# One order table for all engines through batches 0 and 1 of a retention and gated-MLP kernel; q scaled into a buffer of its own, chunk loads in three parts, fixed buffers

## The chip, the core and the metric

The kernel runs on one core of one Trainium2 chip. A core has a matmul engine (TensorE; PE in the profile, its weight loads PEld), a vector engine (VectorE; DVE), an activation engine (ScalarE; ACT), a general engine (GpSimd; POOL) and a sequencer that issues the transfers (SyncE; SP). Each works through its own queue of instructions in order and waits on semaphores for the others. The metric is the time of one execution in microseconds (us), less is better.

## What is computed

Eight batches of 576 positions. First retention: causal scores of eight heads with a decay per head, times v. Then a gated MLP whose gate mixes the positions.

```python
def _attn_ref(q, k, v):                        # [8, 8, 576, 64] each
    scores = scale * np.matmul(q, k.transpose(0, 1, 3, 2))
    gamma = 1.0 - 2.0 ** (-5.0 - np.arange(H))
    rel = pos[:, None] - pos[None, :]
    Dmat = np.where(rel >= 0, gamma[:, None, None] ** rel, 0.0)
    return np.matmul(scores * Dmat, v)
def _moe_ref(x, w_in, w_spatial, b_spatial, w_out):   # x [8, 576, 512]
    h = np.maximum(x @ w_in, 0.0)
    u, v = h[..., :512], h[..., 512:]
    v_n = (v - mean(v)) / np.sqrt(var(v) + 1e-06)
    v_s = np.einsum('ts,bsd->btd', w_spatial, v_n) + b_spatial[None, :, None]
    return (u * v_s) @ w_out
```

## The kernel before

**Precision.** Every wide matmul operand is split into a rounded fp32r part (hi) and a remainder (lo), and a product is three matmuls (`mm3`: hi·hi, hi·lo, lo·hi). The weights arrive as 64-bit floats, seen as pairs of 32-bit words. One block of 128x512 weights takes an absolute value on ACT and a clamp (`front`), three bit operations on DVE (`mid_steps`: shift and mask, two `scalar_tensor_tensor`), a rounding copy on ACT and a subtraction (`back`). There are twelve such blocks: kind 1 (the v half of w_in, by rows), kind 0 (the u half, by columns) and kind 2 (w_out). The spatial weights are split by `w_sp_steps`.

**Stages of a batch.** Retention goes in four chunks of 128 positions and a tail of 64. A chunk has 16 `scores` matmuls (k times q), which DVE multiplies with the decay mask (`mask`, tile `at`); 16 `update` matmuls (k scaled times v), which with POOL's `decay` become the states `sh` and `st`; and `carried` (states times scaled q) and `values` (masked scores times v), which add up in one pair of PSUM banks (`r`). `evac_hi` (ACT) and `evac_lo` (DVE) split that into `x`. Then v (five row blocks, 56 matmuls of 128x512, each with relu, mean and variance on DVE, and a split: tile `vn`), u (96 matmuls of 128x288), vs (112: spatial weights times vn, times u, split into g) and f (96: g times w_out, stored). All but retention share four rotating PSUM banks (`ps_m`, `bufs=4`).

**Scaling.** `prep` multiplies q by `qs` and k by `kd` on POOL, in place; scores and carried both read the scaled q, and the mask holds the inverse power. So scores wait for both multiplications.

**What sets the order.** Up to line 712 every engine follows program order: the calls from line 550 on are the order for batch 0 and part of batch 1, and each engine's queue is that program's instructions for it. A `front`, `prep`, `burst` or `go(v[i])` puts its instructions on several engines at once, so that they stand in one and the same order on all. From line 712 a list scheduler orders the rest; `interleave` (line 530) deals out retention of batch b+1 among the stages of batch b. `load` fetches a chunk of q, k twice (two layouts) and v as one transfer of 1 MB into one of two rotating buffers (chunks 2 and 3 of batch 0 borrow the places of `u` and `wout0`); all transfers are issued by SP in one queue. `spin` runs matmuls on zeros while the first data is under way.

Of the kernel before, what the change touches and what calls it, by code (L numbers as in the profile page):

```python
# [9 lines left out]
F32 = mybir.dt.float32  # L10
# [21 lines left out]

@with_exitstack
def retention_gmlp(ctx, tc, qkv, tails, w_in, w_sp, b_sp, w_out, amask, tmask, qscale, kdec, sdec, out):
    nc = tc.nc
    cp = ctx.enter_context(tc.tile_pool(name="cp", bufs=1))
    ld = ctx.enter_context(tc.tile_pool(name="ld", bufs=2))
    wk = ctx.enter_context(tc.tile_pool(name="wk", bufs=2))
    sp = ctx.enter_context(tc.tile_pool(name="sp", bufs=1))
    ps_r = ctx.enter_context(tc.tile_pool(name="ps_r", bufs=1, space=PSUM))  # L40
    ps_m = ctx.enter_context(tc.tile_pool(name="ps_m", bufs=4, space=PSUM))
# [16 lines left out]
    def slot(name):  # L58
        return cp.tile([P, 2, NCB, S], F32R, name=name, tag="slot", bufs=2)
# [32 lines left out]

    def spin(name, n):
        ps = ps_m.tile([P, 512], F32, name=name, tag="m")
        for i in range(n):
            pe.matmul(ps, idle[:, :P], idle, start=True, stop=True)
# [7 lines left out]
    spin("idle0", 12)  # L104

    tail = {}

    def load(b, c):
        if b == 0 and c in (2, 3):
            tag = ("u", "wout0")[c - 2]  # L110
            t = cp.tile([P, NDB, S] if c == 2 else [P, NDB, DM], F32, name=f"qkv_{b}_{c}", tag=tag)
            t = t.rearrange("p a n -> p (a n)")[:, :4 * 512].rearrange("p (a n) -> p a n", a=4)
        else:
            t = ld.tile([P, 4, 512], F32, name=f"qkv_{b}_{c}", tag="qkv")
        q, k = (t[:, i].rearrange("p (a n) -> p a n", a=NP) for i in range(2))
# [12 lines left out]
    def load_tail(b):
        t = ld.tile([P, 3, NP * TL], F32, name=f"tail_{b}", tag="tail", bufs=1)
        dma(t, tails[b])  # L130
        q, k = (t[:, i].rearrange("p (a n) -> p a n", a=NP) for i in range(2))
        tail[b] = q, k, t[:, 2]

    staged = {}
    early = cp.tile([P, NCB, DH], F32, name="early", tag="vn0")
    raw_v = slot("raw_v").bitcast(I32).rearrange("p i a n -> p (i a n)")

    def fetch(kind, i):
# [3 lines left out]
        else:  # L142
            t = sp.tile([P, 1024], I32, name=f"raw_{kind}{i}", tag="raw", bufs=4)
# [4 lines left out]
    def fetch_wsp():  # L148
        w = slot("raw_s").bitcast(F32).rearrange("p i a n -> p (i a) n")
        for sb in range(NC):  # L150
            dma(w[:, sb], w_sp[sb * P:(sb + 1) * P, :])
        for i in range(2):
            dma(w[i * TL:(i + 1) * TL, NC], w_sp[NC * P:, :])
        dma(w[TL:TL + 1, NC + 1], b_sp)
        staged["s"] = w

    load(0, 0)
    for i in range(2, NCB):
        fetch(1, i)
    dma(sd, sdec)  # L160
    load(0, 1)
    load(0, 2)
    load(0, 3)
    dma(amt, tmask)
    load_tail(0)
    po.memset(vt2.bitcast(F32), 1.0)
    po.memset(wtl[1][TL:].bitcast(F32), 0.0)

    def split(hi, lo, src, eng):
        ac.copy(out=hi, in_=src)  # L170
        eng.tensor_tensor(out=lo, in0=src, in1=hi.bitcast(F32), op=ALU.subtract)

    part = {}

    def front(kind, i, clamp=po):
        words = staged[kind, i].rearrange("p (n two) -> p n two", two=2)
        hw, lw = words[:, :, 1], words[:, :, 0]
        f = early[:, i] if kind == 1 else sp.tile([P, 512], F32, name=f"f_{kind}{i}", tag="f", bufs=3)
        a = f if clamp is po else ps_m.tile([P, 512], F32, name=f"w_{kind}{i}", tag="m")
        ac.activation(out=a, in_=hw.bitcast(F32), func=AF.Abs)  # L180
        if clamp is po:
            po.tensor_scalar(out=a, in0=a, scalar1=2.0 ** -15, scalar2=None, op0=ALU.max)
        part[kind, i] = hw, lw, a, f

    def mid_steps(kind, i):
        hw, lw, a, f = part[kind, i]
        direct = kind == 1 and a is not f
        ps = a if kind != 1 or direct else ps_m.tile([P, 512], F32, name=f"w_{kind}{i}", tag="m")
        part[kind, i] = f, ps
        fi = ps.bitcast(I32)  # L190
        if direct:
            ve.tensor_scalar(out=a, in0=a, scalar1=2.0 ** -15, scalar2=None, op0=ALU.max)
        ve.tensor_scalar(out=fi, in0=a.bitcast(I32), scalar1=3, scalar2=0x3FFFFFFF, op0=ALU.logical_shift_left, op1=ALU.bitwise_and)
        ve.scalar_tensor_tensor(out=fi, in0=hw, scalar=-2 ** 30, in1=fi, op0=ALU.bitwise_and, op1=ALU.bitwise_or)
        yield
        ve.scalar_tensor_tensor(out=fi, in0=lw, scalar=29, in1=fi, op0=ALU.logical_shift_right, op1=ALU.bitwise_or)
        yield

    def mid(kind, i):
        for _ in mid_steps(kind, i):  # L200
            pass

    def back(kind, i, eng=po):
        hi, lo = (w[:, i, DH:] if kind == 1 else w[:, :, i * P:(i + 1) * P] for w in (win if kind < 2 else wout))
        f, ps = (t if kind == 1 else t.rearrange("p (a n) -> p a n", a=NCB) for t in part[kind, i])
        ac.copy(out=hi, in_=ps)
        if eng is po and kind == 1:
            ac.copy(out=f, in_=ps)
        eng.tensor_tensor(out=lo, in0=f if eng is po else ps, in1=hi.bitcast(F32), op=ALU.subtract)

    def w_sp_steps():
        w = staged["s"]
        for sb in range(NC):
# [24 lines left out]

    def prep(b, c):
        q, _, kn, _ = chunk[b, c]  # L240
        q = q.rearrange("p a (s n) -> p a s n", s=2)
        po.tensor_tensor(out=q, in0=q, in1=qs.rearrange("p a (s n) -> p a s n", s=1).broadcast_to([P, NP, 2, D]), op=ALU.mult)
        kh = kn.rearrange("p (h d) -> p h d", h=H)
        po.tensor_tensor(out=kh, in0=kh, in1=kd.broadcast_to([P, H, D]), op=ALU.mult)

    def prep_tail(b):
        q = tail[b][0]
        po.tensor_tensor(out=q, in0=q, in1=qs, op=ALU.mult)
# [23 lines left out]
    def carried(b, c, flip):  # L272
        q = chunk[b, c][0]
# [5 lines left out]
        if c == NC - 1:  # L279
            q = tail[b][0]  # L280
# [21 lines left out]
    def mask(b, c):  # L302
        a = wk.tile([P, 2, NP, D], F32, name=f"at_{b}_{c}", tag="at")
        ve.tensor_tensor(out=a, in0=sc, in1=am, op=ALU.mult)
        at[b, c] = a
# [484 lines left out]
```

## Time and profile before

| | us |
|---|---|
| median of 3 runs (lowest, highest) | 580.56 (580.24, 580.73) |
| the profiled execution's own time | 578.85 |
| its span | 577.1 |
| PE busy in the span | 532.2 (92%), 7247 matmuls |
| DVE, ACT, POOL busy | 244.8, 210.7, 163.0 |
| mean granted PE clock | 0.958 |
| chain of waits that ended last | PE 78%, POOL 8%, DVE 5%, DMA 3% |

An engine that is busy is not always at its full rate: a matmul that runs at half clock is twice as long and just as busy. So PE is read together with its granted clock, and its work is counted in matmuls times their duration at full clock. The profile's tables by stage give both for any stretch.

### The profile page before, as it was taken

The page shows a single profiled execution, that of the slowest core. Times are in us where ns is not written, and L with a number is a line of the kernel's source. Part 1 is how long each engine was busy: PE and PEld are TensorE (multiplying, and loading weights), DVE is VectorE, ACT ScalarE, POOL GpSimd, SP SyncE. Part 2 cuts the span into 40 slices and gives each one's busy share as a digit, 9 for nine tenths or more (in the row PEclk, how much of TensorE's full clock was granted, in tenths as well). Part 3 has the DMA queues.
Part 4 walks back from the last instruction along what each step waited for, and adds up shares of the span by engine and source line. Part 5 has one row for each costly group of instructions (what it writes and reads, how often), then busy time and mean ns, then how long its engine had stood idle before and what let it go on. Part 6 is the DMA issues. An engine that isn't in the chain of part 4 may idle for free.

```text
span 577.1 us, 16334 instructions
## 1 busy us (share of the span) xinstructions
PE 532.2 (92%) x7247; PEld 493.9 (86%) x7247; DVE 244.8 (42%) x586; ACT 210.7 (37%) x479; POOL 163.0 (28%) x173
## 2 busy tenths in 40 slices
PE   5366886898998999999999999999999999999997
PEld 4365676887997989999899989998999989998997
DVE  4524542477034255341735164533734073515350
ACT  3213551256222246223722255223622264225522
POOL 4541765575014232122222322220222222000000
PEclk8577887999999999999999999999999999999999
DMA  8590124510113452222222522242212422010002
GB/s 307 231 352 10 64 76 137 174 49 1 51 40 141 145 188 75 74 88 98 74 76 74 183 75 75 76 141 84 73 48 83 164 76 74 2 64 21 1 1 83
DMA packets 21449, 55.49 MB, mean 96 GB/s; under 512 B 2305, under 2 KB 14849, under 8 KB 17410
## 3 DMA queue, kind: packets, MB, share of 16 engines
q1 hardware_dynamic: 21378, 54.44, 26.9%
q8 instruction: 57, 0.93, 0.7%
q14 instruction: 14, 0.11, 0.1%
HBM read 45.00 MB, written 9.44 MB: 94 GB/s over the span
## 4 chain that ended last, share of the span: by engine, by line
PE 78%; POOL 8%; DVE 5%; DMA 3%; issue 2%; ACT 2%; SPq 0%; ACTq 0%; POOLq 0%; DVEq 0%
PE vs L72 19%; PE f L72 18%; PE u L72 15%; PE v L72 14%; PE r L72 13%; POOL qkv L72 4%; DVE f L72 2%; DMA qkv<-in_qkv 2%; DMA raw_v<-in_w_in 1%; POOL f L72 1%; POOL dec L72 1%; ACT x L72 1%; DVE x L72 1%; DVE st L72 1%; POOL win L72 1%
## 5 line engine op out<-in xcount | busy, mean ns | idle before, releaser
L72 PE MATMUL vs<-wsp,vn 128*128 128x288 f32 x768 | 117.8, 300 | 1.8 <-ACT pre L72 1.8
L72 PEld LDWEIGHTS vs<-wsp,vn 128*128 128x128 f32 x768 | 106.8, 190 | 3.9 <-ACT pre L72 2.0
L72 PE MATMUL u<-x,win 128*128 128x288 f32 x768 | 107.0, 299 | 2.5 <-ACT u L72 2.4
L72 PEld LDWEIGHTS u<-x,win 128*128 128x128 f32 x768 | 104.5, 191 | 4.0 <-ACT u L72 2.7
L72 PE MATMUL v<-win,x 128*128 128x512 f32 x384 | 94.3, 401 | 0.0
L72 PE MATMUL f<-g,wout 128*128 128x288 f32 x672 | 92.8, 296 | 1.0 <-issue 1.0
L72 PEld LDWEIGHTS f<-g,wout 128*128 128x128 f32 x672 | 89.9, 188 | 1.5 <-issue 0.9
L72 PEld LDWEIGHTS v<-win,x 128*128 128x128 f32 x384 | 72.0, 190 | 17.1
L72 POOL TENSOR_TENSOR dec<-sh,sd 128x256 f32<-128x256 f32 x32 | 19.6, 613 | 220.4 <-DVE sh L72 163.6
L72 PE MATMUL r<-qkv 64*64 64x64 f32 x2048 | 43.6, 233 | 26.2 <-POOL qkv L72 25.1
L72 PEld LDWEIGHTS r<-qkv 64*64 64x64 f32 x2048 | 38.2, 146 | 29.8 <-POOL qkv L72 28.8
L72 DVE BATCH_NORM_STATS2 s<-v 128x6 f32<-128x512 f32 (+1 forms) x40 | 27.7, 692 | 71.7 <-ACT v L72 68.2
L72 POOL TENSOR_TENSOR qkv<-qkv,qs 128x512 f32<-128x512 f32 x32 | 41.0, 1282 | 51.7 <-DMA qkv<-in_qkv 42.4
L72 DVE TENSOR_TENSOR vs<-vs,u 128x288 f32<-128x288 f32 x56 | 26.0, 464 | 57.5 <-PE vs L72 57.4
L72 ACT CAST g<-vs 128x288 fp32r<-128x288 f32 x56 | 22.4, 400 | 75.0 <-DVE vs L72 75.0
L72 ACT COPY o<-f 128x288 f32<-128x288 f32 x64 | 25.6, 400 | 62.4 <-PE f L72 57.8
L72 DVE TENSOR_TENSOR at<-r,am 128x512 f32<-128x512 f32 x32 | 22.0, 688 | 59.9 <-PE r L72 59.8
L72 ACT CAST x<-r 128x512 fp32r<-128x512 f32 x32 | 18.7, 586 | 69.4 <-PE r L72 39.9
L72 ACT ACTIVATE u<-u 128x288 f32<-128x288 f32 x56 | 22.8, 407 | 38.5 <-PE u L72 38.3
L72 DVE TENSOR_TENSOR g<-vs,g 128x288 fp32r<-128x288 f32 x56 | 25.5, 456 | 23.0 <-ACT g L72 19.8
L72 DVE TENSOR_TENSOR x<-r,x 128x512 fp32r<-128x512 f32 x32 | 21.9, 685 | 31.5 <-ACT x L72 31.5
L72 POOL TENSOR_TENSOR qkv<-qkv,kd 128x512 f32<-128x512 f32 x32 | 33.4, 1043 | 0.1
(82 smaller groups left out, 615.1 us busy)
## 6 DMA issues: line engine op xcount, KB each, us to landing
qkv<-in_qkv SPq DMA_DIRECT2D x31, 1024.0 KB, 5.0
out<-o SPq DMA_DIRECT2D x64, 144.0 KB, 1.8
tail<-in_tails SPq DMA_DIRECT2D x8, 384.0 KB, 7.0
raw_v<-in_w_in SPq DMA_DIRECT2D x4, 512.0 KB, 6.7
raw<-in_w_in SPq DMA_DIRECT2D x4, 512.0 KB, 9.8
raw<-in_w_out SPq DMA_DIRECT2D x4, 512.0 KB, 3.5
raw_s<-in_w_sp SPq DMA_DIRECT2D x4, 288.0 KB, 3.3
qkv<-in_qkv SPq DMA_DIRECT2D x2, 512.0 KB, 6.6
```

Source lines behind the costliest of these rows:

```text
L72: ins = op(*args, **kw)
```

## The change

The calls that ordered batches 0 and 1 are gone. All their work, with retention of batches 0, 1 and 2 and the first steps of batch 3's, is cut into 188 chains (`scores_chain`, `state_chain`, `burst_chain`, `v_chain`, `weight` and so on), and a string `ORDER` of 612 words names, word by word, which chain takes its next step. A step is mostly one operation on one engine, so the engines' queues are no longer tied to one another call by call. A word also says which engine does a step that either POOL or DVE can do (`w.1.2.vv`: clamp and subtraction on DVE). A string `BANKS` says which of the four PSUM banks each tile of this part gets. From batch 2 on the scheduler and `interleave` work as before.

Further: `prep_q` writes the scaled q to a buffer `qsc`, so that scores read q as it was loaded, and the mask (`am`) now holds the decay of the difference; for a batch's first chunk only the half that is needed is scaled. A chunk's transfer is three (q and k, k by position, v), into two, two and three fixed buffers, and it is issued one chunk earlier. A weight block's last bit operation writes from PSUM to an SBUF tile, from which the rounding copy and the subtraction read; the extra ACT copy of `back` is gone. All tiles are allocated once by name (`keep`); tags that were shared by rotation are now named places (`lent`).

```diff
+ORDER = """
+    D.1.0 z.0.12 D.1.2 d.0.0 d.0.0 w.1.0.vp w.1.0.vp c.a c.k w.1.0.vp D.1.1 w.1.2.vv g.0.0 d.0.0 k.0.0.p c.q
...
+BANKS = "012301320103012130230230030230202123123132323020121312002131232123102313"
...
+    def keep(name, shape, dtype=F32, tag=None):
+        if name not in kept:
+            kept[name] = cp.tile(shape, dtype, name=name, tag=tag or name)
+        return kept[name]
...
+            n = b * NC + c + (0 if b else 2)
+            qk = keep(f"qk{n % 2}", [P, 2, 512])
+            kn = keep(f"kn{n % 2}", [P, 512])
+            vv = keep(f"vv{n % 3}", [P, 512])
...
+            parts = (qk, qkv[b, c, :, :2]), (kn, qkv[b, c, :, 2]), (vv, qkv[b, c, :, 3])
...
+        ve.scalar_tensor_tensor(out=f.bitcast(I32), in0=lw, scalar=29, in1=fi, op0=ALU.logical_shift_right, op1=ALU.bitwise_or)
+        yield
+        ac.copy(out=at_hi(), in_=form(f))
+        yield
+        last.tensor_tensor(out=at_lo(), in0=form(f), in1=at_hi().bitcast(F32), op=ALU.subtract)
...
+    def prep_q(b, c, eng=po):
+        q = chunk[b, c][0].rearrange("p a (s n) -> p a s n", s=2)
+        t = keep(f"qsc{c % 2}", [P, NP, 2, D])
...
+        r = slice(1 if c == 0 else 0, 2)
+        eng.tensor_tensor(out=t[:, :, r], in0=q[:, :, r], in1=w.broadcast_to([P, NP, 2 - r.start, D]), op=ALU.mult)
...
-        q = chunk[b, c][0]
+        q = scaled[b, c]
...
+    def state_chain(b, c, e1=po, e2=po):
+        update(b, c)
+        yield
+        if c == 0:
+            ac.copy(out=sh, in_=ds[:, 0])
+        else:
+            ve.tensor_tensor(out=sh, in0=ds[:, 0], in1=dec[0], op=ALU.add)
+        yield
+        decay(dec[1], sh, e1)
...
+    def run(order):
+        for name in order.split():
+            chain = chains.get(name)
+            if chain is None:
+                head, *rest = name.split(".")
+                chain = chains[name] = makers[head](*rest)
+            next(chain)
...
-    for b in range(1, B):
-        interleave(main(b), retention(b + 1) if b + 1 < B else [], 50.0 if b > 1 else 26.1, 12.5 if b > 1 else 13.25)
+    for b in range(2, B):
+        interleave(main(b), retention(b + 1) if b + 1 < B else [], 50.0, 12.5)
...
-    dec = scale * gamma[None, :, None] ** -both[:, None, None].astype(np.float64)
-    am = np.where(j[None, :] >= both[:, None], 1.0, 0.0)[:, None, :] * dec
+    rel = j[None, :] - both[:, None]
+    dec = gamma[None, :, None] ** np.maximum(rel, 0)[:, None, :]
+    am = np.where(rel[:, None, :] >= 0, scale * dec, 0.0)
```

The matmuls at the program's start, before. `idle` is the zero work of `spin`, `r_99` the PSUM pair of scores and updates, `r_98` that of carried and values, `qkv_0_115` and `qkv_1_126` the first two chunks (their scores and updates are the rows of 32); the first v matmul comes behind another 64 matmuls, of chunks 1 and 2.

```order
L72 MATMUL idle_100<-wsp_80 128x512 x12
L72 MATMUL r_99<-qkv_0_115 64x64 x32
L72 MATMUL idle_206<-wsp_80 128x512 x3
L72 MATMUL r_98<-qkv_0_115,sh 64x64 x4
L72 MATMUL r_99<-qkv_1_126 64x64 x32
L72 MATMUL r_98<-qkv_0_115,sh 64x64 x4
L72 MATMUL r_98<-at_0_171,qkv_0_115 64x64 x16
```

The same place now. `qk_111` and `qk_167` are the q and k of chunks 0 and 1 as loaded, `kn` and `vv` the scaled k and v, `qsc` the scaled q, `slot_214` is x of batch 0, `m_92` a PSUM bank.

```order
L128 MATMUL m_89<-wsp_71 128x512 x12
L128 MATMUL r_94<-qk_111 64x64 x16
L128 MATMUL r_94<-vv_113,kn_112 64x64 x16
L128 MATMUL m_92<-wsp_71 128x512 x3
L128 MATMUL r_93<-qsc_172,sh 64x64 x8
L128 MATMUL r_93<-at_145,vv_113 64x64 x16
L128 MATMUL r_94<-qk_167 64x64 x16
L128 MATMUL r_94<-vv_169,kn_168 64x64 x16
L128 MATMUL m_92<-win_69,slot_214 128x512
L128 MATMUL m_92<-win_70,slot_214 128x512
```

Chunk 0's carried and values have moved ahead of chunk 1's scores and updates, scores no longer read a scaled buffer, and the first v matmuls stand right behind chunk 0's part of x.

DVE from its first weight work on, before. `w_138`, `w_151`, `w_189` and `w_278` are the four kind 1 blocks, `early` the SBUF place that POOL clamps, `x_137` is x of batch 0.

```order
L72 TENSOR_SCALAR w_138<-w_138 128x512 x2
L72 SCALAR_TENSOR_TENSOR w_138<-raw_v,w_138 128x512 x2
L72 TENSOR_SCALAR w_151<-early 128x512
L72 SCALAR_TENSOR_TENSOR w_151<-raw_v,w_151 128x512 x2
L72 TENSOR_TENSOR at_0_171<-r_99,am 128x512
L72 TENSOR_TENSOR st_88<-r_99,dec_91 128x256
L72 TENSOR_SCALAR w_189<-w_189 128x512 x2
L72 SCALAR_TENSOR_TENSOR w_189<-raw_v,w_189 128x512 x2
L72 TENSOR_TENSOR x_137<-r_98,x_137 128x2x4x64
```

DVE behind its first ten rows now. `lent_vn_95` is the place that was `early`, `lent_slot_96` the raw words, `m_89` and `m_91` PSUM banks, `dec` a decayed state, `qsc_233` chunk 1's scaled q.

```order
L128 SCALAR_TENSOR_TENSOR lent_vn_95<-lent_slot_96,m_90 128x512
L128 TENSOR_SCALAR lent_vn_95<-lent_vn_95 128x512
L128 TENSOR_SCALAR m_89<-lent_vn_95 128x512
L128 TENSOR_TENSOR dec_82<-sh,sd 128x256
L128 SCALAR_TENSOR_TENSOR lent_vn_95<-lent_slot_96,m_91 128x512
L128 TENSOR_TENSOR st_79<-r_94,dec_82 128x256
L128 TENSOR_TENSOR qsc_233<-qk_167,qs 128x512
L128 SCALAR_TENSOR_TENSOR m_89<-lent_slot_96,m_89 128x512
```

The blocks are now woven into one another and into chunk 0's steps, and DVE has work that POOL did: clamps, decays, a scaling of q, later subtractions.

More of the change, by code (lines that the diff above doesn't have):

```diff
@@ L1 @@
+import itertools
 import math
@@ L91, in retention_gmlp, with bank @@
     ve.memset(idle.bitcast(F32), 0.0)
+    banks = itertools.chain((int(k) for k in BANKS), itertools.cycle(range(4)))
+    bank_tiles = [ps_m.tile([P, 512], F32, name=f"m{i}") for i in range(4)]
+    def bank():
+        return bank_tiles[next(banks)]
     def spin(name, n):
-        ps = ps_m.tile([P, 512], F32, name=name, tag="m")
+        ps = bank()
         for i in range(n):
@@ L164, in retention_gmlp, with of_weight, weight @@
[L164 to L175, printed above, removed]
+    def of_weight(kind, i, n):
+        w = win[n] if kind < 2 else weight_of_out(n)
+        return w[:, i, DH:] if kind == 1 else w[:, :, i * P:(i + 1) * P]
+    def weight(kind, i, least=po, last=po):
@@ L185, in mid_steps @@
[L185 to L189, printed above, removed]
+        f = early[:, i] if kind == 1 else keep(f"f{(2 * kind + i) % 3}", [P, 512])
+        at_hi, at_lo = (lambda n=n: of_weight(kind, i, n) for n in range(2))
+        form = (lambda t: t) if kind == 1 else (lambda t: t.rearrange("p (a n) -> p a n", a=NCB))
@@ L394, in retention @@
             states(b, 0)
+        if (b, 2) not in chunk:
+            load(b, 2)
         yield 0.95
@@ L403, in retention @@
             after(b, c, nx)
[L404 to L405 removed]
+            if nxt[c + 3][0] < B and nxt[c + 3] not in chunk:
+                load(*nxt[c + 3])
             if c == 0 and b not in tail:
@@ new lines, in dma_one, with dma_chunk, dma_tail, dma_wsp @@
+    def dma_one(dst, src):
+        dma(dst, src)
+        yield
+    def dma_chunk(b, c):
+        parts = []
+        load(b, c, parts)
+        for part in parts:
+            part()
+            yield
+    def dma_tail(b):
+        load_tail(b)
+        yield
+    def dma_wsp():
+        w = lent("slot1", [P, 2, NCB, S]).rearrange("p i a n -> p (i a) n")
+        staged["s"] = w
+        for sb in range(NC):
+            dma(w[:, sb], w_sp[sb * P:(sb + 1) * P, :])
+            yield
+        for i in range(2):
+            dma(w[i * TL:(i + 1) * TL, NC], w_sp[NC * P:, :])
+        dma(w[TL:TL + 1, NC + 1], b_sp)
+        yield
@@ new lines, in once, with scores_chain @@
+    def once(f, *args):
+        f(*args)
+        yield
+    def scores_chain(b, c):
+        scores(b, c)
+        yield
+        mask(b, c)
+        yield
+    def state_chain(b, c, e1=po, e2=po):
+        update(b, c)
+        yield
+        if c == 0:
+            ac.copy(out=sh, in_=ds[:, 0])
+        else:
+            ve.tensor_tensor(out=sh, in0=ds[:, 0], in1=dec[0], op=ALU.add)
+        yield
+        decay(dec[1], sh, e1)
+        yield
+        new = st[(c + 1) % 2]
+        ve.tensor_tensor(out=new, in0=ds[:, 1], in1=dec[1], op=ALU.add)
+        yield
+        if c + 1 < NC:
+            decay(dec[0], new, e2)
+            yield
@@ new lines, in first, with first_u, vs_chain @@
+    def first():
+        return lent("wout1", [P, NDB, DM])
+    def first_u(t):
+        ps = bank()[:, :HALF]
+        u_mm(0, 0, t, ps)
+        yield
+        ac.activation(out=first()[:, t, :HALF], in_=ps, func=AF.Relu)
+        yield
+    def vs_chain(t, db):
+        ts = slice(t * HALF, (t + 1) * HALF)
+        ds = slice(db * P, (db + 1) * P)
+        ps = bank()[:, :HALF]
+        for sb in range(NC):
+            mm3(ps, [normed(i)[:, sb, ds] for i in range(2)], [wsp[i][:, sb, ts] for i in range(2)], sb == 0, False)
+            if db == 0 and t == 0:
+                yield
+        pe.matmul(ps, vt1[:, ds], wtl[0][:, ts], start=False, stop=False)
+        pe.matmul(ps, vt2[:TL + 33, ds], wtl[1][:TL + 33, ts], start=False, stop=True)
+        yield
@@ L712, in retention_gmlp, with main @@
+    def main(b):
+        for chain, cost in stages(b):
+            for _ in chain:
+                pass
+            yield cost
     ordered[0] = False
```

628 lines of the change are left out of this document (288 added, 340 removed).

## Prediction

> **What bounds the kernel now.** I first read the page's busy shares, then the tables by stage over stretches that end where PE passes from one part of the work to the next.
>
> ```profile
> PE 532.2 (92%) x7247; PEld 493.9 (86%) x7247; DVE 244.8 (42%) x586; ACT 210.7 (37%) x479; POOL 163.0 (28%) x173
> ...
> 5.40:33.40 28.00, 12.93 (x312) 10.58 (x311) 13.31 (x21) 6.63 (x15) 15.84 (x15) 0.57 0.79 297
> 33.40:77.40 44.00, 31.98 (x404) 26.18 (x401) 19.98 (x52) 18.89 (x39) 22.28 (x21) 0.81 0.30 106
> 77.40:147.70 70.30, 60.45 (x803) 55.65 (x803) 38.09 (x80) 29.66 (x62) 40.16 (x35) 0.95 0.26 89
> 147.70:211.20 63.50, 61.31 (x1051) 57.22 (x1049) 19.90 (x44) 16.32 (x43) 15.96 (x19) 1.00 0.34 112
> 211.20:274.40 63.20, 63.20 (x905) 59.43 (x905) 27.20 (x68) 23.69 (x56) 14.75 (x17) 1.00 0.27 93
> ```
>
> The columns are PE, PEld, DVE, ACT and POOL busy us, granted clock, DMA share and GB/s. From 211.2 on PE is never idle, at full clock: no order can make that part shorter. Before 77.4 it is idle 27.1 of 72 us, at a clock of 0.57 and 0.81, so the loss sits at the start. What PE's work costs at full clock I take from the chain of waits: the last batch's v, u, vs and f, and a stretch of retention.
>
> ```profile
> 413.25 2.02 PE r L72 x128
> ...
> 520.49 13.03 PE v L72 x56
> 533.52 12.73 PE u L72 x96
> 546.25 14.88 PE vs L72 x112
> 561.13 12.74 PE f L72 x96
> ```
>
> That is 233 ns for a v matmul, 133 for u, vs and f, and 15.8 ns for one record of retention, of which a matmul has two. Why PE waits at the start is told by the timeline:
>
> ```profile
> 7.93 1.49 POOL L72 TENSOR_SCALAR early<-early 128x512 f32<-128x512 f32 x1 [6.05 <-ACT early L72]
> 9.39 1.26 POOL L72 TENSOR_TENSOR qkv<-qkv,qs 128x512 f32<-128x512 f32 x1
> ...
> 17.30 1.49 POOL L72 TENSOR_SCALAR early<-early 128x512 f32<-128x512 f32 x1
> 18.75 1.26 POOL L72 TENSOR_TENSOR qkv<-qkv,qs 128x512 f32<-128x512 f32 x1
> ...
> 20.07 2.13 PE L72 MATMUL r<-qkv 64*64 64x64 f32 x64 [4.03 <-POOL qkv L72]
> ...
> 33.36 3.06 PE L72 MATMUL v<-win,x 128*128 128x512 f32 x12
> ...
> 77.45 0.46 DVE L72 TENSOR_TENSOR u<-vs,pre 128x288 f32<-128x288 f32 x1 [1.18 <-PE vs L72]
> ```
>
> POOL clamps weights ahead of scaling q, and PE's scores wait for it; the first v matmul comes at 33.4, the first vs tile is taken up at 77.45. No engine is full meanwhile: DVE is busy 33.3 of the 72 us to 77.4, POOL 38.1. The bound is the order, a chain that hops between half-empty engines.
>
> **The first part of the change: up to the first vs tile (A).** The new order has 95 DVE instructions from its first clamp to the product with that tile. Their durations by shape:
>
> ```profile
> L72 DVE SCALAR_TENSOR_TENSOR vn<-v,sm,vn 128x512 fp32r<-128x512 f32 x32 | 23.8, 744 | 6.5 <-ACT vn L72 6.4
> L72 DVE BATCH_NORM_STATS2 s<-v 128x6 f32<-128x512 f32 x32 | 22.2, 693 | 70.5 <-ACT v L72 67.3 <-ACT r L72 2.5
> L72 DVE TENSOR_TENSOR at<-r,am 128x512 f32<-128x512 f32 x32 | 22.0, 688 | 59.9 <-PE r L72 59.8
> L72 DVE SCALAR_TENSOR_TENSOR f<-raw,f 128x512 int32<-128x512 int32 x16 | 14.0, 876 | 0.4
> L72 DVE TENSOR_TENSOR st<-r,dec 128x256 f32<-128x256 f32 x32 | 13.5, 423 | 27.1 <-POOL dec L72 27.0
> L72 DVE TENSOR_SCALAR sm<-sm 128x1 f32<-128x1 f32 x64 | 13.3, 208 | 1.5
> L72 DVE BATCH_NORM_AGGREGATE mv<-s 128x2 f32<-128x6 f32 x32 | 5.7, 178 | 0.6
> L72 DVE SCALAR_TENSOR_TENSOR w<-raw_v,w 128x512 int32<-128x512 int32 x8 | 5.6, 696 | 0.3
> L72 DVE TENSOR_SCALAR f<-f 128x512 int32<-128x512 int32 x8 | 5.0, 625 | 3.7 <-POOL f L72 3.7
> ```
>
> 16 bit operations at 0.69 (now through PSUM, as the row of `w`) make 11.1; 6 clamps at 0.625, 3.8; 6 masks and 5 `evac_lo` at 0.69, 7.6; 10 state sums and 2 small tail operations at 0.42, 5.1; 6 means and variances at 0.87, 5.2; 20 one-column operations at about 0.2, 3.9; 5 splits of vn at 0.744, 3.7; two products, 1.2; and, taken over from POOL, 4 small (decays and a tail scaling) at 0.42 and 7 wide ones at 0.69, 6.5. Sum 48.1 us of DVE, against POOL's 29 by the same count and PE's 33: **DVE becomes the bound of A**.
>
> When does it start? The first weight block is on DVE at 5.4 as before. For the rest I go by bytes:
>
> ```profile
> 10.00:12.00 2.00, 1.13 (x32) 0.94 (x32) 1.63 (x4) 0.07 (x1) 1.88 (x3) 0.50 1.01 408
> ...
> 20.00:22.00 2.00, 1.93 (x66) 1.88 (x68) 0.00 (x0) 0.00 (x0) 1.01 (x2) 0.50 1.01 374
> ...
> qkv<-in_qkv SPq DMA_DIRECT2D x1, 1024.0 KB, 8.5
> ```
>
> Chunk 1 was issued at 7.5 and landed 8.5 us later, at 16.0, as byte 4.59 million; at 0.41 MB a us the new order's pieces land: chunk 0's q and k 8.3, its other k 9.0, its v 11.5 (after a weight block), chunk 1's q and k 13.3, the fourth weight block 15.3, chunk 1's v 16, chunk 2 at 18.4. Followed by hand with the durations above: chunk 0's scores at 8.4, updates at 11.6, its x by 17.6, so the first v matmuls at about 18 instead of 33.4; DVE ends the fourth block's subtraction (15.3 us of its 48.1) near 23.0, some 2 us late for waiting on that block. The other 32.8 us follow with PE, ACT and POOL ahead of it most of the time; I add 3 us for waits and contention: 58.8, taken as 58.6 with the last product still running. Bounds: rows on DVE overlap by about 0.07 us, so 95 of them without any wait end at 5.4+48.1-6.6 = 47; above, the port (next) could add 19.
>
> **The port.** Work that goes from POOL to DVE has two SBUF inputs, and the trace shows what can happen then. These are DVE bit operations with both inputs in SBUF: one beside a pair of POOL subtractions, two alone, two beside another such pair; and a POOL pair that had little DVE work beside it:
>
> ```profile
> 60.05 0.66 DVE L72 SCALAR_TENSOR_TENSOR f<-raw,f 128x512 int32<-128x512 int32 x1
> ...
> 107.46 1.42 DVE L72 SCALAR_TENSOR_TENSOR f<-raw,f 128x512 int32<-128x512 int32 x2
> ...
> 118.87 3.64 DVE L72 SCALAR_TENSOR_TENSOR f<-raw,f 128x512 int32<-128x512 int32 x2
> ...
> 58.66 3.36 POOL L72 TENSOR_TENSOR wsp<-raw_s,wsp 128x576 fp32r<-128x576 f32 x2
> 65.44 2.83 POOL L72 TENSOR_TENSOR wsp<-raw_s,wsp 128x576 fp32r<-128x576 f32 x2
> ...
> 118.51 3.44 POOL L72 TENSOR_TENSOR x<-u,x 128x576 fp32r<-128x576 f32 x2
> ```
>
> At 118.87 they take 1.82 us each instead of 0.71; at 60.05 DVE is as fast as alone, and POOL is 0.27 slower each. The mean of the 16 is 876 ns against 696 for those through PSUM: +0.18 on the average, +1.1 at worst. A has 11 moved operations and 6 clamps: 17 x 0.18 = 3.1 us (my 3 us), 17 x 1.1 = 19 at worst. The change also takes 16 operations off this risk, since all bit operations now read PSUM. [...]
>
> **The second part: from there to 211.2 (B).** Before it took 133.8 us. PE's work in it, by the order's counts: 210 vs, 168 u, 192 f at 0.133 (75.8), 80 v at 0.233 (18.6), 600 retention matmuls at 0.0316 (19.0): 113.4. So 20.4 were lost. The new order has done more by the end of its first vs tile (12 v matmuls and some 60 of retention, 4.7 us), leaving 108.7. DVE has 73 us in that stretch by the same durations, so PE is the bound. I take 8 us of bubbles: less than half of the 20.4, since DVE is still two-thirds full and shares the cover; between 2 and 20.4. A and B: 58.6+108.7+8 = 175.3.
>
> **The rest.** From that point both orders hold the same matmuls (24 v of batch 2 done; 32 v, then u, vs, f and retention in nearly the same sequence, some u tiles later). It took 577.1-211.2 = 365.9, PE full, so I leave it: 365.9, give or take 2. Unscaled scores, transfers in three parts and the halved first scaling change no PE count; SP's added issues lie beside PE, and would cost only if stores came to wait behind a load's buffer. Fixed buffers follow the same rotation as the pools; I price them at nothing, covered by PE's backlog, and at most at a bubble in B. The copies of `early` that go were beside DVE's work:
>
> ```profile
> L72 ACT COPY early<-w 128x512 f32<-128x512 f32 x3 | 1.8, 601 | 0.0
> ```
>
> **Sum.** 175.3+365.9 = 541.2 of span, against 577.1: 35.9 less. The profiled execution's own time is 1.75 above its span and 1.7 below the median, so I take 35.9 off the median: 544.7, say **544.5**.
>
> **The rivals.** *Denser* (0.13): no waits in A (53.5) and 2 us of bubbles: 11 more, 533. For it, ACT and POOL have 33 and 29 us of work in A's 48; against, a step still hops between three engines. *Half of it* (0.19): a fixed order holds everything behind a step that is late, so that A ends at 65 and B loses 20.4 as before: 18.8 back, 563. For it, PE's clock was 0.57 to 0.81 where it idled, and at half clock A's 33 us of matmuls alone would take 66. *Slower* (0.04): the port. The order has 35 moved two-input operations up to batch 2; if each paid the worst 1.1 us and all lay on the path, 38.5 us would be added and the time 583; it decides from 1.0 us each. Against it: POOL loses the same work, and most of B has PE as cover. *Nothing changes* (0.02): stores queued on SP behind loads in the steady part take back what the start gives, 6 us a batch. Against it, from the list of waits (total, times, longest):
>
> ```profile
> ACT o L72 <- DMA out<-o: 4.5, 3, 1.6
> ```
>
> **Chances.** My forecast (537 to 553) 0.62; the others as given. About 0.2% is what a measurement of this kernel can tell from no change. Faster 0.94, within 0.02, slower 0.04. For 8 in 10 the range takes most of the denser case and about half of the half case: 534 to 562.
>
> **What would show it.** Right: first v matmuls near 18, first vs tile taken up at 55 to 62 with DVE over 75% busy from 18 to then, the 24th v matmul of batch 2 and the retention behind it done near 175 with PE idle under 10 us from 60 on, then 63.2 us a batch. Wrong in A: DVE idle a third of the time, or DVE's `dec` and `win` rows well over 0.42 and 0.69. Wrong in B: PE waiting on DVE products or on PSUM banks. Wrong in the rest: a period other than 63.2, or ACT's `o` copies waiting for stores.

## The result and the profile after

The change gives 547.08 us (median of 4 runs, 544.84 to 552.5) against 580.44 beside it (4 runs): ratio 0.9438, interval 0.9362 to 0.9515. The forecast was 544.5 in a range of 534 to 562. The profiled execution took 548.99 us with a span of 547.2, so its span is 29.9 shorter than that of before, where 35.9 was forecast; that execution was 1.9 above the median.

The page's busy shares, then the table by stage, cut where the prediction cut it (first v matmul, first vs tile taken up by DVE, the 24th v matmul of batch 2 with the retention behind it). Columns as before: span, PE, PEld, DVE, ACT and POOL busy, granted clock, DMA share, GB/s.

```profile
PE 522.8 (96%) x7247; PEld 485.7 (89%) x7247; DVE 269.3 (49%) x627; ACT 207.4 (38%) x476; POOL 117.3 (21%) x132
```

```profile
5.40:18.95 13.55, 9.00 (x184) 6.81 (x183) 10.72 (x17) 4.53 (x9) 6.57 (x6) 0.68 1.00 364
18.95:65.50 46.55, 38.09 (x724) 30.79 (x728) 38.43 (x78) 23.01 (x49) 27.26 (x27) 0.95 0.62 209
65.50:179.85 114.35, 109.69 (x1668) 103.78 (x1657) 68.68 (x150) 41.78 (x99) 20.25 (x19) 0.99 0.37 115
179.85:247.20 67.35, 67.35 (x922) 62.80 (x921) 28.37 (x71) 25.26 (x59) 15.29 (x19) 0.99 0.29 93
247.20:311.00 63.80, 63.80 (x909) 59.90 (x908) 28.09 (x72) 24.14 (x57) 14.17 (x18) 1.00 0.30 95
```

PE has the same 7247 matmuls and is idle for 24.4 us instead of 44.9. A ends at 65.5 (forecast 58.6), B at 179.85 (175.3), and what follows takes 367.35 (365.9). So the miss of 6 us is A's: +6.9, then -2.3 and +1.4. The timeline of PE, with one row of DVE, shows where A was held up. A row: start, duration, engine, operation, count, and in brackets the idle time ahead of it and what ended it.

```profile
18.88 0.79 PE L128 MATMUL m<-win,slot 128*128 128x512 f32 x1
...
27.36 0.27 PE L128 MATMUL r<-qsc,st 64*64 64x64 f32 x1 [0.22 <-issue]
...
28.93 0.63 PE L128 MATMUL r<-lent_wout 64*64 64x64 f32 x26
34.39 0.49 PE L128 MATMUL r<-lent_wout 64*64 64x64 f32 x6 [4.84 <-issue]
34.80 5.67 PE L128 MATMUL m<-win,slot 128*128 128x512 f32 x18
...
65.39 0.42 DVE L128 TENSOR_TENSOR u<-m,lent_wout 128x288 f32<-128x288 f32 x1
```

The first v matmul starts at 18.9, as forecast (18). But PE stops for 4.84 us after 26 of the 32 records of the update of chunk (0,3), and nothing that the profile names ended that stop ("issue"). The table in 2 us steps shows what follows:

```profile
30.00:32.00 2.00, 0.00 (x0) 0.00 (x0) 1.64 (x4) 1.15 (x3) 0.82 (x1) 1.00 1.00 244
32.00:34.00 2.00, 0.00 (x0) 0.00 (x0) 0.00 (x0) 0.00 (x0) 1.61 (x2) 1.00 0.84 216
34.00:36.00 2.00, 1.61 (x9) 1.30 (x10) 1.00 (x3) 0.00 (x0) 0.12 (x1) 0.52 0.36 116
36.00:38.00 2.00, 2.00 (x8) 1.54 (x7) 0.36 (x2) 0.28 (x1) 0.00 (x0) 0.63 0.01 5
```

From 32 to 34 DVE and ACT stand too, since they wait for PE; and when PE goes on, its clock is granted at half until 37.5. A little later, in the timelines of DVE (first row) and POOL:

```profile
46.83 4.24 DVE L128 TENSOR_TENSOR wsp<-lent_slot,wsp 128x576 fp32r<-128x576 f32 x1
```

```profile
45.83 1.45 POOL L128 TENSOR_TENSOR wsp<-lent_slot,wsp 128x576 fp32r<-128x576 f32 x1
47.23 0.61 POOL L128 TENSOR_TENSOR dec<-st,sd 128x256 f32<-128x256 f32 x1
47.80 1.44 POOL L128 TENSOR_TENSOR wsp<-lent_slot,wsp 128x576 fp32r<-128x576 f32 x1
49.20 1.26 POOL L128 TENSOR_TENSOR qsc<-qk,qs 128x512 f32<-128x512 f32 x1
50.41 1.13 POOL L128 CAST slot<-xt 128x512 fp32r<-128x512 f32 x1
```

One subtraction on DVE lasts 4.24 us. It begins beside the first of four POOL operations with two SBUF inputs that follow one another without a pause, and it ends at 51.07, 0.6 us behind the last of the four (50.46); alone such a subtraction takes 0.74 (below). In B there is one large gap. SP, ACT and PE around it, from their timelines:

```profile
166.10 7.26 SPq L128 DMA_DIRECT2D out<-o  x5
173.40 0.45 SPq L128 DMA_DIRECT2D vv<-in_qkv  x1
...
171.32 0.70 ACT L128 COPY o<-m 128x288 f32<-128x288 f32 x2 [5.25 <-DMA out<-o]
...
177.51 1.13 PE L128 MATMUL r<-vv,kn 64*64 64x64 f32 x32 [3.84 <-issue]
```

The v of chunk (3,1) is the last word of the table. SP came to it only after five stores, and the stores waited for ACT's copies, which waited for an earlier store. It was issued at 173.40, and PE's update went on 4 us later.

### The profile page after: what moved, and what is told of

The parts are those of the page before. It is cut to its first block, busy times and chain, and to the rows that moved or that the text cites. A ratio compares the mean times of both kernels' runs of the same rounds, so it can differ in the third digit from the quotient of the medians.

```text
span 547.2 us, 16422 instructions
## 1 busy us (share of the span) xinstructions
PE 522.8 (96%) x7247; PEld 485.7 (89%) x7247; DVE 269.3 (49%) x627; ACT 207.4 (38%) x476; POOL 117.3 (21%) x132
## 4 chain that ended last, share of the span: by engine, by line
PE 87%; DVE 7%; issue 3%; DMA 1%; ACT 1%; SPq 0%; DVEq 0%; ACTq 0%
PE m L128 75%; PE r L128 12%; DMA am<-in_amask 1%; DVE wsp L128 1%; DVE m L128 1%; DVE slot L128 1%; DVE sm L128 1%; DVE s L128 1%; DVE at L128 1%; SPq L128 0%; DVE u L128 0%; DVE kn L128 0%; DVE st L128 0%; DVE f L128 0%; DVE vn L128 0%
## 5 line engine op out<-in xcount | busy, mean ns | idle before, releaser
L128 PE MATMUL m<-wsp,vn 128*128 128x288 f32 x768 | 115.5, 297 | 0.5 <-DVE f L128 0.5
L128 PE MATMUL m<-slot,win 128*128 128x288 f32 x768 | 107.7, 296 | 0.1
L128 PEld LDWEIGHTS m<-wsp,vn 128*128 128x128 f32 x768 | 106.1, 188 | 1.7 <-DVE f L128 0.6
L128 PE MATMUL m<-slot,wout 128*128 128x288 f32 x768 | 106.2, 296 | 0.8 <-issue 0.6
L128 PEld LDWEIGHTS m<-slot,win 128*128 128x128 f32 x768 | 104.0, 188 | 1.9 <-issue 0.5
L128 PEld LDWEIGHTS m<-slot,wout 128*128 128x128 f32 x768 | 102.6, 188 | 2.0 <-issue 0.8
L128 PE MATMUL m<-win,slot 128*128 128x512 f32 x384 | 97.1, 405 | 0.8 <-ACT lent_wout L128 0.8
L128 PEld LDWEIGHTS m<-win,slot 128*128 128x128 f32 x384 | 72.1, 192 | 17.5 <-ACT lent_wout L128 1.1
L128 POOL TENSOR_TENSOR qsc<-qk,qs 128x512 f32<-128x512 f32 (+1 forms) x25 | 29.3, 1171 | 184.1 <-PE r L128 163.6
L128 PE MATMUL r<-qsc,sh 64*64 64x64 f32 x512 | 28.7, 230 | 0.3 <-ACT r L128 0.3
```

Source lines behind the costliest of these rows:

```text
L128: ins = op(*args, **kw)
```

## The experiments

All are variants of the changed kernel unless said otherwise; times are medians beside the kernel before. "First vs" is when DVE takes up the first vs tile, "mark" the end of B; both, the early stop of PE and the stretch of half clock that goes with it (from the clock records) are of the one profiled execution.

| | us (lowest, highest) | ratio and interval | early stop | half clock | first vs | mark | span |
|---|---|---|---|---|---|---|---|
| the change, again | 549.51 (547.95, 550.78) | 0.9458 [0.9398, 0.9518] | 4.95 | 33.1 to 39.9 | 66.15 | 179.6 | 547.9 |
| q alone, on before | 573.06 (572.61, 573.84) | 0.9884 [0.9863, 0.9905] | 2.71 | none | 72.88 | | 570.8 |
| scaled scores | 547.85 (545.88, 549.29) | 0.9443 [0.9416, 0.947] | none | none | 65.19 | 176.4 | 544.0 |
| moved work back on POOL | 551.04 (547.15, 552.02) | 0.9473 [0.9406, 0.954] | 4.50 | 37.4 to 44.2 | 68.51 | 181.4 | 549.8 |
| parts at once | 557.84 (557.07, 558.59) | 0.9603 [0.9561, 0.9645] | 4.22 | 34.5 to 38.0 | 65.66 | 189.6 | 556.3 |
| spatial sums on POOL | 544.08 (539.68, 546.03) | 0.9356 [0.9284, 0.9427] | 2.37 | none | 59.68 | 171.0 | 537.7 |
| spatial sums on DVE | 546.87 (544.54, 549.11) | 0.9417 [0.9373, 0.9462] | 1.72 | none | 61.87 | 174.7 | 542.4 |
| 16 matmuls more in front | 551.18 (547.62, 553.16) | 0.9496 [0.945, 0.9542] | 3.29 | 35.2 to 42.0 | 68.74 | 181.1 | 547.5 |
| v load earlier | 543.59 (542.8, 546.58) | 0.9369 [0.9295, 0.9444] | 3.37 | 33.6 to 37.0 | 64.59 | 175.1 | 541.8 |
| POOL sums + v load | 541.77 (538.25, 545.7) | 0.9342 [0.929, 0.9394] | 4.51 | 33.5 to 40.3 | 64.48 | 174.1 | 543.6 |
| the same, spatial loads late | 542.02 (540.29, 544.36) | 0.9337 [0.9294, 0.938] | 4.84 | 32.2 to 39.1 | 64.24 | 174.7 | 542.3 |
| POOL sums + v load, 64 matmuls in front | 538.15 (535.36, 541.19) | 0.9256 [0.9214, 0.9299] | 0.34 | none | 60.66 | 171.5 | 536.3 |

**The change again**, as the measure for the others.

> The changed kernel again, word for word. Its four runs so far lie between 544.8 and 552.5 us, far wider than those of the kernel before. Theory 1: the two stalls in which PE waits for nothing that the profile shows (4.84 us at 29.6 and 3.84 us at 173.7) are of different kinds; the one at 173.7 waits for the v part of a chunk's load and comes back in every profile within 0.5 us, the one at 29.6 is a matter of when PE's instructions arrive and changes its length from run to run. Theory 2: both are fixed by the program and come back alike; then the scatter must show elsewhere, as DVE rows of other lengths. Median 545 to 549 by both.

Its early stop came at the same matmul, 4.95 us long. A kernel's runs lie 1 to 8 us apart here, so a difference under about 3 us is not read from medians alone.

**The q part: alone on the kernel before, and taken out of the change.**

```diff
 # on before: scores read the q as loaded
-        po.tensor_tensor(out=q, in0=q, in1=qs..., op=ALU.mult)
+        t = wk.tile([P, NP, 2, D], F32, name=f"qsc_{b}_{c}", tag="qsc", bufs=2)
+        po.tensor_tensor(out=t, in0=q, in1=qs..., op=ALU.mult)
```

```diff
 # on the change: scores read the scaled q, the old mask; in the table c.q goes
 # to the front and seven q words ahead of the scores of their chunk
-        q, k, _, _ = chunk[b, c]
+        k, q = chunk[b, c][1], scaled[b, c]
```

In the second edit a batch's first chunk is scaled whole again, since its scores need all of it.

> The kernel before, with one part of the change alone: scores take unscaled q and the mask of the change, and the scaled q lies in a buffer of its own; the order of before is kept. Theory O (the order carries the gain): within 3 us of before, 577 to 583, since DVE and PE follow the same order and only a wait for the scaling of about 1 us goes in some chunks. Theory Q: a third of the gain or more, 569 us or less.

> The part of the change that takes scores from unscaled q is undone: scores read the scaled q again, with the mask of before, and q's scaling stands ahead of the scores in the table. Theory O (the order of the table carries the gain): a later first score by one scaling of a chunk, 1.0 to 1.3 us on POOL or DVE in four places of A, of which DVE's own queue hides a part: 0 to +4 us against the unchanged kernel, 548 to 554. Theory Q (the gain hangs on q's own buffer and on scores that do not wait for the scaling): at least a third of the gain is lost, 560 us or more, and PE waits for the scaled q show in the list of waits with several us each.

Alone it is worth 7.4 us, 22% of the change's gain, between what the two theories gave. The lists of PE's waits (engine, tile, releaser: total, times, longest) of before, of q alone, and of the change with scaled scores:

```profile
PE r L72 <- POOL qkv L72: 25.1, 10, 4.8
```

```profile
PE r L72 <- POOL qkv L72: 8.1, 5, 3.5
```

```profile
PE r L127 <- POOL qsc L127: 8.7, 3, 3.9
```

In the old order 17 us of waiting for POOL go, and two thirds of that comes back as other waits, among them a stop of 2.71 us to 42.47 that again nothing ends ("issue"). In the new order, taking the part out brings 8.7 us of waiting back and the time stays: with one of these waits (3.92 us, to 25.75) PE comes later to the place of the early stop, and does not stop there. That wait has a stretch of half clock of its own, from 24.1 to 30.9. So the change keeps its gain without the unscaled scores, but the wait stands here in the place of the stop; what they are worth where there is no stop is not shown.

**The engines' letters: all of the work that a letter moved from POOL to DVE back on POOL**, 149 words (44 operations), in the same order.

```diff
-    w.1.0.vp w.1.0.vp c.a c.k w.1.0.vp D.1.1 w.1.2.vv
+    w.1.0.pp w.1.0.pp c.a c.k w.1.0.pp D.1.1 w.1.2.pp
```

> All operations that the order moved from POOL to DVE (clamps, decays, scalings, subtractions, 149 words) are on POOL again; the order of the words is kept. Theory 1 (DVE is the bound up to the first vs tile, so moving work to it was a cost, not a gain): DVE has 9 us less there, the first vs tile comes 2 to 6 us sooner. Theory 2 (the moves shorten chains that hop to POOL, where a wide operation takes 1.0 to 1.5 us instead of 0.7 and waits in a queue): POOL goes from 29 to 45 us of work there, the first vs tile comes 3 us or more later, and the time rises by 3 to 12 us.

```profile
18.95:68.51 49.56, 40.40 (x750) 32.54 (x748) 29.24 (x70) 24.37 (x51) 41.51 (x41) 0.88 0.61 197
```

The time is the same within the scatter. DVE now has 29.2 us of work in this stretch and POOL 41.5, instead of 38.4 and 27.3. So DVE's load, on which the prediction's A rests, can be shed without a gain: POOL takes its place, and PE's early stop is there too.

**The parts of a load: all three issued where the first stands.**

```diff
         for part in parts:
             part()
+        for part in parts:
             yield
```

> The loads of a chunk in three parts at three places of the table are undone: all three parts are issued where the first part stands, in the order of the change otherwise. Theory O (the order of the engines carries the gain, the parts only let SP pass a busy buffer): between -3 and +6 us against the unchanged kernel, 546 to 555, with the v of chunk (3,1) no longer behind the stores, so its stall of 1.7 to 3.8 us at 170 to 180 gone. Theory L (the parts carry a good deal of it, because a part whose buffer is still in use now holds up every load behind it on SP): 560 or more, with PE's waits for qk, vv or kn at 5 us and more.

Some parts now come ahead of the last products that read the chunk in the same buffer, and those products take the newer k or v; the amount of work is the same. It costs 8 us against the change (0.9603 to 0.9458, intervals apart), just past theory O's bound. PE waits once for 5.8 us for a v, and once for 4.4 us ("issue") ahead of an update; all of the cost lies behind the first vs, since the mark comes 123.9 us after it instead of 113.4. So in this table the parts carry about a quarter of the gain. The bulk, some 20 us, is neither q nor parts nor letters. That leaves the order and what no run took out by itself: the fixed buffers, the weight steps through PSUM without the copies of `early`, and the bank table. That it is the order is argued by elimination, not shown.

**Contention of POOL and DVE: the spatial sums all on POOL, or all on DVE.**

```diff
-s.1.v s.1.v s.3.v s.4.v s.3.v s.4.v
+s.1.p s.1.p s.3.p s.4.p s.3.p s.4.p
```

```diff
-s.0.p s.2.p s.5.p s.5.p s.2.p s.0.p
+s.0.v s.2.v s.5.v s.5.v s.2.v s.0.v
```

> The five subtractions of the spatial weights are all on POOL instead of three on DVE, two on POOL; nothing else changes. In the changed kernel the three took 1.07, 4.24 and 1.05 us on DVE, against 0.69 by my prediction. [...]

> All six pairs of the spatial sums on DVE (the change has three there and three on POOL), the opposite of the run that put all six on POOL. Theory P (a DVE operation that reads two SBUF tensors is held up while POOL runs such operations back to back: 4.24 us in place of 0.69): with POOL's wsp rows gone, no wsp row of DVE is over 2.6 us, their mean is 1.3 or less, and DVE's six take less than the 5.3 us of the three before plus 1; the time is 546 to 551, since DVE's added 2 to 3 us stand against 3 us less of holding up. Theory T (the row is long for a reason of its own, its tile or its place): the row at that place is still about 4.2, and the time 550 to 554.

DVE's timeline with all six on DVE:

```profile
42.65 0.74 DVE L127 TENSOR_TENSOR wtl<-lent_slot,wtl 64x576 fp32r<-64x576 f32 x1
43.31 0.74 DVE L127 TENSOR_TENSOR wsp<-lent_slot,wsp 128x576 fp32r<-128x576 f32 x1
...
44.65 1.17 DVE L127 TENSOR_TENSOR wsp<-lent_slot,wsp 128x576 fp32r<-128x576 f32 x1
...
46.56 1.01 DVE L127 TENSOR_TENSOR wsp<-lent_slot,wsp 128x576 fp32r<-128x576 f32 x1
```

Such a subtraction takes 0.74 us where POOL waits, 1.0 to 1.2 beside one or two operations of POOL, and 4.24 in the change beside a row of four: theory P holds. The long row came back in all five other profiles that keep POOL's four together (4.20 to 4.78 us). What decides that DVE waits for a whole row, and not for one operation, is not shown: the subtraction of 1.17 us at 44.65 stood beside two POOL operations without a pause between them. This lengthening of DVE's rows beside POOL's is what the prediction calls the port; by what the two hold one another up is not shown either. What it costs the kernel is less than the row. Between the change again and POOL sums + v load, which stop for nearly as long (4.95 and 4.51), the first vs comes 1.7 us earlier, of which 0.4 is the stop. So the port is worth some 1.2 us of A, by one profile each. With the sums on POOL alone the first vs comes 6.5 us earlier; the rest of that is the shorter stop in its profile (2.6) and the full clock behind it (18 wide matmuls in 4.5 us instead of 6.9).

**The early stop: is it PE's own instructions?** Sixteen small matmuls on zeros are added in front:

```diff
+        for i in range(16 if n == 3 else 0):
+            pe.matmul(ps[:, :64], idle[:, :P], idle[:, :64], start=True, stop=True)
```

> Sixteen small matmuls on zeros (128x64) are added to the idle matmuls that PE does ahead of the first projection, where it waits for data anyway, so that every later PE instruction has a place 16 matmuls higher in PE's program. In four runs the early stall of PE (2.4 to 5.0 us, put down to issue) came at the same matmul, the 27th of the 32 of the update of chunk (0,3), whatever the time was. Theory I (the stall belongs to a place in PE's own instructions, not to data): it comes 16 matmuls earlier, at the 11th of the 32, and is about as long, 2.4 to 5.0 us. Theory W (a wait for data, a buffer or a bank that the records do not name): it stays in front of the 27th. By both the time is within 2 us of the unchanged kernel, since the added work lies in idle time.

```profile
32.45 0.39 PE L127 MATMUL r<-lent_wout 64*64 64x64 f32 x10
36.13 0.91 PE L127 MATMUL r<-lent_wout 64*64 64x64 f32 x22 [3.29 <-issue]
```

The stop moved from 26 of the 32 to 10 of the 32, by exactly 16: it belongs to a place in PE's program and not to data. Counted from the start, by the tables by stage, 475 matmuls stand ahead of the stop in the change and in this run, and in every other profile that has it, q alone in the old order among them. (The time is 1.7 us above the change again; the added matmuls took about 0.2 us each, more than the idle time there.) The DMA view points to the cause. It lists the queues with packets, MB and the share of 16 engines; for the change from 31.6 to 31.8 us, and for this run from 33.6 to 33.8:

```profile
q8 instruction: 1, 0.02, 37.4%
```

```profile
q8 instruction: 1, 0.02, 34.6%
```

A queue of kind "instruction" begins one packet there, 2.6 and 2.5 us ahead of the matmul that ends the stop. Over the whole span it has 57 packets and 0.93 MB, so 16 KB each; 57 times 128 matmuls are 7296, just over the kernel's 7247. In the change the two stops of 27.36 and 34.39 stand 127 records apart (5 of q and states, 32 and 16 of scores, 16 of q and states, 32 of values, then 26), a matmul and a weight load each; one record may be missing. By these counts PE's instructions arrive in blocks of about 128 matmuls with their weight loads, one packet each; ahead of the long stop PE ran such a block, all of it 64x64 matmuls of 16 ns each, in 2.2 us, while the packet with the next one went through DMA engines whose share was 1.00 to 1.05 from 20 to 32 us.

Then two attempts to be rid of it, both on top of POOL sums + v load (below). The first moves four of five steps of the spatial loads later, so that less is asked for ahead of the packet:

```diff
-    S t.0.v ... S b.0.2 m d.1.0 ... S v.0.1 ... S v.0.1 ... s.1.p ... s.2.p ... S s.1.p ... d.1.0 p.1.0.pp s.5.p
+    S t.0.v ... b.0.2 m d.1.0 ... v.0.1 ... v.0.1 ... S s.1.p ... S s.2.p ... s.1.p ... d.1.0 p.1.0.pp S S s.5.p
```

> On top of the two edits that were run together (541.8 us): four of the five steps that load the spatial weights (1.15 MB less in front) stand later in the table, the second just ahead of its first reader, the third likewise, the last two behind the third part of chunk (1,0). Theory I2: PE's early stall is its own next instructions, fetched by the same DMA engines behind the data already asked for (the instruction queue's packet in this stretch lands 2.4 to 2.8 us ahead of the matmul that ends the stall, in six runs with 16 matmuls' shift among them); with less data asked for before 27 us the packet lands earlier, the stall falls under 2.5 us, PE's granted clock does not drop to 0.50 behind it, and the first vs tile's product comes at 59 to 61, the median 536 to 540. Theory F (the packet comes at a fixed lead of PE's own progress, whatever the queues carry): stall of 4 to 5 us as before, half clock behind it, 541 to 544. If the spatial weights now come too late, ACT waits for lent_slot around 38 us, and the gain is gone by that wait.

No effect: 4.84 us of stop, half clock behind it, the same median. The engines' share was 1.04 until 30 us all the same, since the other loads fill it. That leaves open how far the packet's delay follows the load on the queues. The second puts the blocks' ends elsewhere:

```diff
-        for i in range(n):
+        for i in range(8 if n == 12 else n):
             pe.matmul(ps, idle[:, :P], idle, start=True, stop=True)
+        for i in range(68 if n == 12 else 0):
+            pe.matmul(ps[:64, :64], idle[:64, :64], idle[:64, :64], start=True, stop=True)
```

> The two edits that were run together (spatial sums on POOL, the v of chunk (3,1) earlier; 541.8 us), and four of the twelve wide idle matmuls at PE's start replaced by 68 small ones on zeros (64x64), so that every later PE instruction stands 64 matmuls further on. Theory I (PE's instructions come in blocks of 128 matmuls with their weight loads, one packet of the instruction queue each; in the trace of the change the stalls of 0.22 us at 27.36 and of 4.84 us at 34.39 stand 127 matmul records apart, and the next block lands some 6 to 7 us after the block before it was begun): the blocks now end amid wide matmuls, which last longer than the fetch; no stall above 1.5 us between 25 and 45 us, a granted clock of 1.00 there, the 18 wide matmuls behind the update of chunk (0,3) in 4.5 us instead of 5.7 to 6.9, the first vs tile's product at 58 to 60, the median 535 to 539. Theory W (the stall is owed to what stands there, or the whole of this stretch is bound by the loads): it comes again near the update of chunk (0,3), 3 us or more, and the time stays at 541 to 544.

PE's timeline and its table by stage:

```profile
32.10 0.27 PE L127 MATMUL r<-qsc,sh 64*64 64x64 f32 x1 [0.34 <-issue]
...
33.31 4.47 PE L127 MATMUL m<-win,slot 128*128 128x512 f32 x18
```

```profile
24.00:30.00 6.00, 5.37 (x126) 4.57 (x127) 5.83 (x8) 2.56 (x5) 4.64 (x4) 1.00 1.03 397
30.00:36.00 6.00, 5.66 (x158) 4.54 (x157) 5.84 (x12) 3.27 (x8) 5.81 (x8) 1.00 0.68 211
```

The stop is now at a state matmul after 10 of 16, which is 64 records ahead of the old place (26 + 32 + 6), again behind 475 matmuls, and it is 0.34 us long. The 18 wide matmuls take 4.47 us, and DVE is busy 97% from 24 to 36: in this stretch DVE is now the bound (from the first v matmul to the first vs it is busy 34.02 of 39.3 us, 87%). At 538.15 us this is the fastest kernel of the study, faster than the change by more than the intervals (0.9256 [0.9214, 0.9299] against 0.9458 [0.9398, 0.9518]). One thing more differs: the idle matmuls now last until 12.6, so that the first scores start 4 us later and PE has hardly any idle time at its start (busy 17.39 of the first 20 us). That did not make the start faster. The view's clock of 1.00 ahead of 23.9 does not fit the durations there: 32 records of scores take 1.13 us at 12.60 (0.69 at full clock), and three wide matmuls 1.65 at 21.36 (0.96 at full clock in the run with 16 matmuls more), so PE ran at half rate although it was hardly ever idle. The first v matmul comes at 21.36 instead of 18.62 in POOL sums + v load, and from there to the first vs it takes 39.3 us instead of 45.9. Of these 6.6 us the shorter stop is 4.2 and the 18 wide matmuls at full clock 2.5. So in these two profiles the gain is the stop and the clock behind it, less 2.7 us lost at the start.

**The load of chunk (3,1): its v right behind its k**, alone and together with the sums on POOL.

```diff
-    F.1.1.3 d.3.1 p.2.3.vp ... F.1.1.0 p.3.0.vv d.3.1
+    F.1.1.3 d.3.1 d.3.1 p.2.3.vp ... F.1.1.0 p.3.0.vv
```

> The last word of the order, the load of v for the second chunk of batch 3, stands behind the load of that chunk's other k, some 40 words earlier and ahead of six stores of batch 1. Theory 1: PE's stall of 3.84 us at 173.7 is a wait for this load, which SP issued at 173.4 behind stores that waited for ACT; it goes, and the time falls by 3.5 to 5 us, with the mark (the 24th v matmul of batch 2 and the retention behind it) at 175 to 176.5 instead of 179.9. Theory 2: the stall is PE's instruction stream: it stays, within 1 us, and so does the time.

> Both edits that each gave about 5 us alone, together: the spatial products and their sums on POOL instead of DVE, and the third part of chunk (3,1) issued right behind its second part. If the two act in different stages (the first in A, the second in B at the mark) they add up: 549.5 - 5.4 - 5.9 = 538 us, between 536 and 541. If both only moved the kernel about within its scatter of 3 to 5 us, or if the second only lets the first stall come out at another place, the sum is not reached and the time is 543 to 547. In the profile: first vs tile's product at 59 to 61, no wait of PE for the v of chunk (3,1), the mark at 166 to 170.

SP's timeline with the earlier word:

```profile
162.90 0.33 SPq L127 DMA_DIRECT2D vv<-in_qkv  x1
163.32 0.38 SPq L127 DMA_DIRECT2D tail<-in_tails  x1
165.30 7.37 SPq L127 DMA_DIRECT2D out<-o  x5
172.98 0.34 SPq L127 DMA_DIRECT2D qk<-in_qkv  x1
```

The stores still take 7.4 us on SP, but no load of chunk (3,1) is behind them, PE's wait for it is gone, and the mark comes 110.5 us after the first vs instead of 113.4 (the change again). The two edits together give 7.7 us over the change again, less than the 11.3 of both alone. In the profiles the difference is the early stop (2.37 us at full clock with the sums on POOL, 4.51 and half clock here); whether it is so in the medians too is not shown, since the profiled execution of the former was the fastest of its four and that of the latter the slowest.

## Why the prediction was right, and where its sum was off

- **The mechanism** was the order, and the runs do not contradict it: with q, the parts or the letters taken out one by one, the time moves by -1.7, +8.3 and +1.5 us against the change again, the first and the last within the scatter. That the rest is the order is argued by elimination, as said above. The forecast did not divide the gain among these.
- **How near it was** is in part luck: the median is 2.6 us above the forecast, but the profiled span 6.0 above its sum, and there an A that was too short stands against bubbles in B that were too many.
- **The start** came as worked out by bytes: first v matmul at 18.9 (18).
- **A, mis-sized by +6.9** (65.5 instead of 58.6). The term that failed is the 3 us for waits and port. From 5.4 to 65.5 DVE was busy 49.15 us, near the 48.1 of the sum (its rows overlap by some 0.07 us each and clamps took some 0.43 instead of 0.625, which makes up for the port), but idle 10.95, where 2 for the fourth block and the 3 were allowed; by the table in 2 us steps 5.0 of the idle time lie between 30 and 38, at PE's stop and in the half clock behind it. The stop took 4.84 us of PE, the half clock about 1.2 (18 wide matmuls in 5.67 us instead of 4.46), and the port some 1.2 (above). "DVE becomes the bound" was half right: DVE was 83% busy from 18.95 to 65.5, over the 75% named, but with its load moved to POOL nothing was gained; only without the stop was DVE full, and only for a stretch. Where stop and clock were small, A ended at 59.7, 60.7 and 61.9.
- **The port** was priced at 0.18 on the average and 1.1 at worst for an operation; one row paid 3.5 over 0.74, the other moved rows of A at most 0.9. The groups of DVE's operations by shape (busy, mean ns):

```profile
L128 DVE TENSOR_TENSOR wsp<-lent_slot,wsp 128x576 fp32r<-128x576 f32 x2 | 5.3, 2657 | 0.0
L128 DVE TENSOR_TENSOR kn<-kn,kd 128x512 f32<-128x512 f32 x4 | 3.4, 855 | 0.0
...
L128 DVE TENSOR_TENSOR qsct<-tail,qs 128x256 f32<-128x256 f32 x2 | 2.3, 1130 | 0.0
```

  Against 0.69 and 0.42 these are +2 us, +0.17 and +0.7 each. The longest, 4.24 against 0.74, stood beside POOL's row of four. The rival that made the kernel slower by such rows needed 1.0 us more on each of 35 operations; here one row paid more than that.
- **B, -2.3**: 8 us of bubbles were allowed, and PE was idle for 4.7, of which 3.84 was one load behind stores. That is the mechanism of the rival "nothing changes", in one place instead of every batch:

```profile
ACT o L128 <- DMA out<-o: 9.6, 3, 5.3
```

- **The rest, +1.4**: PE is busy 362.1 of 367.35 us, before 361.6 of 365.9, so it was never quite full; 1.0 of the 1.4 is idle time, and the start lies in half clock until 180.9. The period is as forecast: the row of 63.8 us holds 909 matmuls and that of 63.2 before 905, and four at 0.133 make most of the difference.
- **Half of it** was near in A (it put A's end at 65) but not in B, which lost 4.7 and not 20.4.

## What to carry to other kernels

When every wait that the profile names is short and the program is still late, look at the idle time that nothing ends: here PE ran 127 records of tiny matmuls in 2.2 us and then stood for 4.84, with the next instruction packet beginning 2.6 us before it went on, and 16 added idle matmuls showed it by moving the stop by 16. Place the ends of such blocks elsewhere, so that wide matmuls stand among a block's tiny ones: here that took the stop from 4.51 to 0.34 us. And in a table that orders all engines, read SP's words as a queue: a load whose word stands behind stores is as late as the stores (here behind five of them, 7.26 us on SP, and PE stood for 3.84).

## What was not expected of the hardware

PE waited for its own instructions, 1.7 to 5.0 us behind its 475th matmul in ten profiles of this kernel and its variants, with the instruction packet beginning 2.3 to 2.8 us before PE went on, however long the stop was.

Stops of 1.72 and 2.37 us at that place left the clock at 1.00; those of 3.29 to 4.95 went with a stretch at 0.50, which lasted 3.4 or 6.8 us in every case. The length of a stop alone does not decide: in B a stop of 2.24 us (spatial sums on DVE, to 172.4) and one of 2.77 (the change again, to 177.2) went with half clock, one of 2.72 (16 matmuls more, to 179.7) did not. The half clock cost the 18 wide matmuls 1.2 to 2.5 us. What brings the half clock on is not shown.

Why the stop is 2.37 us in one variant and 4.95 in another with the same PE instructions up to there stays open, and so does whether it makes the scatter of 1 to 8 us among runs of one kernel. The runs that were only timed have no trace, but a mean clock: in the change the run of 552.5 us has 0.972 and the three others 0.981 to 0.983, and in the variants with the sums on POOL or the v load earlier the slowest run has the lowest clock too. Where in the span it was lost they do not say.
